# Startup edits and a table of per-stage offsets in the instruction order of a two-layer attention and feed-forward kernel

## The chip, the core and the metric

The kernel runs on one core of one Trainium2 chip. The metric is the device time of one execution in microseconds (us). A program on this core is five instruction queues that run side by side: TensorE (PE in the profile, with its weight loads as PEld), VectorE (DVE), ScalarE (ACT), GpSimd (POOL) and SyncE (SP, which here only issues DMAs). Each queue is worked off in the order in which it was written; an instruction whose inputs are late holds up everything behind it in its own queue.

## What is computed

A sequence of 2048 tokens of width 640 goes through four layers: attention with a memory (A), a feed-forward layer (B), A again, B again, with the same weights both times. Every layer normalises its input first and adds its result to it.

```python
x = A_x
x = x + _A_ref(_layernorm(x, axis=-1), A_wq, A_wk, A_wv, A_wo, A_beta)
x = x + _B_ref(_layernorm(x, axis=-1), B_w1, B_w2)
x = x + _A_ref(_layernorm(x, axis=-1), A_wq, A_wk, A_wv, A_wo, A_beta)
x = x + _B_ref(_layernorm(x, axis=-1), B_w1, B_w2)
# in _A_ref, for each of 4 segments of 512 tokens, 32 heads of width 20:
logits = jnp.einsum('bhqd,bhkd->bhqk', qs, ks) * scale + mask
p = _softmax(logits, axis=-1)
a_dot = jnp.einsum('bhqk,bhkd->bhqd', p, vs)
num = jnp.einsum('bhld,bhde->bhle', pq, M)      # pq = phi(qs), phi(t) = t+1 or exp(t)
den = jnp.einsum('bhld,bhd->bhl', pq, z)[..., None] + 1e-06
o = g * (num / den) + (1.0 - g) * a_dot          # g = sigmoid(beta), one value per head
M = M + jnp.einsum('bhld,bhle->bhde', phi(ks), vs)
z = z + jnp.einsum('bhld->bhd', phi(ks))
```

B is `relu(x @ w1) @ w2` with an inner width of 1728.

## The kernel before

**Tiles and stages.** Tokens lie on the 128 partitions, 16 tiles of 128 tokens (`x_sb`). A stage is named by a layer number a (0 or 1) and a segment s (0 to 3). For each stage the kernel normalises (statistics on DVE, `stats`; the power -0.5 on POOL, `chain`, L700 to L711; the scaling on DVE), turns the tiles so that features lie on partitions (a DMA transpose, `turn`, except for the first segment, which TensorE turns), projects to q, k and v (`proj_part`, `proj_v`), spills q and k to DRAM and loads them back as four heads per group at partitions 0, 32, 64, 96 (`spill`, `fill`), computes scores on TensorE with 20-row tiles (`scores`, L1170, "rows" mode), exponentials on ACT (`exps`, L1235, 128 x 1024 each), the causal mask on POOL (`causal`), the weighted sum of values (`apply`), a DMA transpose and a division on DVE (`divide`, L1359), the memory read and write (`mem_read`, `mem_write`), the sum of the two terms (`combine`, L1388), another DMA transpose (`turn_o`), the output projection (`out_proj`), a second normalisation (`ln_b`, L1442) and the feed-forward layer (`ffn`, `ffn_rest`).

**Who sets the order.** All these stages are Python generators ("streams") that are added in a fixed sequence at L1566 to L1602, so that each has a number n: 0 `scores`, 1 `exps`, 2 `causal`, 5 `turn_pair`, 6 `divide`, 7 `turn_o`, 8 and 9 `out_proj`, 10 and 11 `ln_b`, 12 `fill`, 13 `spill`, 14 `combine`, 15 and 16 `phi_`, 17 and 18 `mem_read`, 19 `turn_k`, 20 `mem_write`, 25 the fourth `first_one`, 26 `first_ln_b`, 27 `proj_ln`, 29 and 30 `proj_one`, 31 `proj_v`, 32 `ffn`, 33 `ffn_rest`, 34 `store`, 36 `consts`, 37 `loads`, 38 `late_loads`. Streams that go through the eight stages carry the rank 4a + s; others keep rank 0. When the program is built, `Sched.run` (L298) repeatedly looks at the next instruction of every stream, estimates with built-in costs when it could start, and appends to its engine's queue the one with the smallest key (L334):

```python
key = (round(start + late), 0.5 if op.urgent else prio, self.rank[id(st[1])], n)
```

`start` is the later of the engine's estimated free time and the inputs' estimated arrival; `late` is a reserve that `_late` (L275) adds from some point on for inputs that have only just come. The order in the queues is fixed by this when the program is built; on the chip only real arrivals count. An engine can't skip an instruction that was appended too early.

**The first 20 us.** Four x tiles are loaded, tiles 0 and 1 by SP, tiles 2 and 3 by ACT. `warm_pe` (L646) runs 52 matmuls of 128 columns on the identity matrix, which POOL has built before. Tiles 0 and 1 get mean and variance on DVE (`first_sums`, L782) and a chain of two POOL instructions each; tiles 2 and 3 get them on ACT (`first_ln_b`, L800: two sums, one mean, two sums of squares), then one DVE instruction that scales the sums (in `chain`, recorded as L708), then the power on POOL. `first_tile` (L756) normalises each tile on DVE, turns it with five TensorE transposes (L764) into a PSUM bank, and copies it out (L771 or L773). Then the projections of the first segment run (L673 in `group`). `MISC` (L484) is four PSUM banks that nearly all stages share.

**Constants.** `consts` (L592) lets POOL build the mask `maskg` (a memset and ten selections), loads beta for all 128 partitions by one SP DMA of 128 rows (L627), takes its exponential on ACT (L630) and derives the gate on DVE (L631 to L641).

Of the kernel before, what the change touches and what calls it, by code (L numbers as in the profile page):

```python
# [5 lines left out]
dt = mybir.dt  # L6
ACT = mybir.ActivationFunctionType
# [3 lines left out]
D = 640  # L11
H = 32
# [160 lines left out]
HOLDERS = 1  # L173
HOLD_TOL = {"pe": 220.0, "act": 150.0, "dve": 200.0, "pool": 0.0, "sp": 0.0}


class Sched:
# [120 lines left out]
    def run(self):  # L298
        while True:
# [24 lines left out]
            for prio, n, st, alts, op, late in heads:  # L324
# [9 lines left out]
                key = (round(start + late), 0.5 if op.urgent else prio, self.rank[id(st[1])], n)  # L334
# [94 lines left out]
def bass_interleave_layers__memory_aug_infini_attn__dense_activation_relu__prompt_kernel(  # L429
    nc, A_x, A_wq, A_wk, A_wv, A_wo, A_beta, B_x, B_w1, B_w2, out,  # L430
):
    with contextlib.ExitStack() as es:
# [13 lines left out]
        ident = sb("ident", [128, 128])  # L446
        warm = sb("warm", [128, 1], dt.float32)
        asum = sb("asum", [128, 4], dt.float32)
        beta_bc = sb("beta_bc", [128, H])
# [3 lines left out]
        stats6 = sb("stats6", [128, 12, 2, 6], dt.float32)  # L453
# [19 lines left out]
        om_sb = sb("om_sb", [128, NJ, D])  # L473
        rden = sb("rden", [128, 2, 2, NJ, 4, 1], dt.float32)
# [58 lines left out]
        def loads():  # L533
# [7 lines left out]
            for t in range(4):  # L541
                yield from ld(("sp", "act")[t // 2], "x0%d%d" % divmod(t, 2), 163840, lambda e, t=t: e.dma_start(
                    x_sb[:, t, :], xs[:, t, :]))
            yield from cols("wk0", wk_r, A_wk, 0, 256)
# [47 lines left out]
        def consts():  # L592
            tw = yield dve(4, 1, lambda e: e.memset(warm[:], 0.0))
            yield act(4, lambda e: e.activation(warm[:], warm[:], ACT.Exp), [tw], psum=False)
            t0 = yield pool(150, lambda e: e.memset(ident[:], 0.0))
            t1 = yield pool(250, lambda e: e.affine_select(
                out=ident[:], in_=ident[:], compare_op=ALU.not_equal, fill=1.0, base=0,
# [16 lines left out]
            t3 = yield pool(700, lambda e: e.memset(maskg[:], 1.0))  # L614
            tmm = []
            for c in range(FC):
# [9 lines left out]
            yield Need("x11")  # L626
            tb = yield dma("sp", sem_("d_beta"), 16384, lambda e: e.dma_start(  # L627
                beta_bc[:], bass.AP(tensor=A_beta.tensor, offset=A_beta.offset, ap=[[0, 128], [1, H]])))
            yield Need("stg", 0, 0, 0, 1)
            te = yield act(32, lambda e: e.activation(gt[:, 0, :], beta_bc[:], ACT.Exp), [tb], psum=False)  # L630
# [14 lines left out]

        def warm_pe():  # L646

            idt = yield Need("ident")
            yield Acq([X])
            tk = yield pe(4600.0, [(lambda e: e.matmul(  # L650
                ps[:, 0, 0:128], ident[:], ident[:], start=True, stop=True), k == 51) for k in range(52)], idt)
            X.release(tk)

# [37 lines left out]
        def stats(t, xt):  # L691
            tk = None
            for c2 in range(2):
                tk = yield dve(320, 1, lambda e, c2=c2: e.bn_stats(  # L694
                    stats6[:, t % 12, c2, :], x_sb[:, t, c2 * 320:(c2 + 1) * 320]), xt)
            tk = yield dve(50, 1, lambda e: e.bn_aggr(
                mv[:, t, :], stats6[:, t % 12, :, :].rearrange("p c s -> p (c s)")), [tk])
# [938 lines left out]
```

## Time and profile before

| What | Value |
|---|---|
| Time, median of 3 runs | 556.43 us (555.3 to 559.99) |
| Span of the profiled execution, first to last instruction | 553.7 us |
| That execution's own time | not listed apart from the three runs: the span is 1.6 us under the lowest and 2.7 us under the median |
| PE busy | 545.7 us, 8340 matmuls |
| DVE / ACT / POOL busy | 414.2 / 408.7 / 191.9 us |
| PE's share of the chain that ended last | 89% |
| Granted TensorE clock, mean | 1.000 |

The span is the time between the first and the last instruction; the times of the runs include what lies around it. A busy PE is not a PE at its peak: every matmul's record includes the time until its result has left the array, about 0.17 us more than what it costs in a dense stream (a 128 x 512 matmul has a mean of 380 ns on the page, and eight of them in a row took 1.89 us at 95.66 us, one every 216 ns).

### The profile page before, as it was taken

The page shows a single profiled execution, that of the slowest core. Times are in us where ns is not written, and L with a number is a line of the kernel's source. Part 1 is how long each engine was busy: PE and PEld are TensorE (multiplying, and loading weights), DVE is VectorE, ACT ScalarE, POOL GpSimd, SP SyncE. Part 2 cuts the span into 40 slices and gives each one's busy share as a digit, 9 for nine tenths or more (in the row PEclk, how much of TensorE's full clock was granted, in tenths as well). Part 3 has the DMA queues.
Part 4 walks back from the last instruction along what each step waited for, and adds up shares of the span by engine and source line. Part 5 has one row for each costly group of instructions (what it writes and reads, how often), then busy time and mean ns, then how long its engine had stood idle before and what let it go on. Part 6 is the DMA issues. An engine that isn't in the chain of part 4 may idle for free.

```text
span 553.7 us, 19086 instructions
## 1 busy us (share of the span) xinstructions
PE 545.7 (99%) x8340; PEld 308.3 (56%) x8340; DVE 414.2 (75%) x1059; ACT 408.7 (74%) x518; POOL 191.9 (35%) x302
## 2 busy tenths in 40 slices
PE   8999999999999999999999999999999999999998
PEld 7464554455564555646446555565456654657756
DVE  5967989897898988997687998669886886417202
ACT  5699889889877888687887887778874878651140
POOL 5245344343444334343433443034430433301000
DMA  8595999933854138466276332971439322342201
GB/s 271 134 232 158 227 186 211 239 72 45 191 112 91 32 58 199 79 93 92 60 188 107 60 69 21 207 147 22 67 48 223 92 36 54 69 81 28 74 2 51
DMA packets 130292, 61.32 MB, mean 111 GB/s; under 512 B 109090, under 2 KB 120098, under 8 KB 130210
## 3 DMA queue, kind: packets, MB, share of 16 engines
q1 hardware_dynamic: 129648, 59.58, 50.8%
q8 instruction: 65, 1.06, 0.8%
q10 hardware_dynamic: 562, 0.53, 0.3%
q14 instruction: 17, 0.14, 0.1%
HBM read 20.57 MB, written 12.85 MB: 60 GB/s over the span
## 4 chain that ended last, share of the span: by engine, by line
PE 89%; DVE 5%; DMA 2%; ACT 2%; POOL 0%; SPq 0%; issue 0%; ACTq 0%; POOLq 0%
PE ps L673 42%; PE ps L676 27%; PE ps L1192 8%; PE ps L1286 6%; ACT PT L1254 2%; PE ps L1325 1%; PE ps L1072 1%; PE ps L650 1%; DMA oT<-o_sb 1%; DMA otk<-otu 1%; PE ps L1466 1%; PE ps L1129 1%; DVE hT L1490 1%; DVE xn_tok L740 1%; DMA beta_bc<-in_A_beta_dram 1%; DVE o_sb L1380 1%
## 5 line engine op out<-in xcount | busy, mean ns | idle before, releaser
L1254 ACT ACTIVATE PT<-ps 128x1024 bf16<-128x1024 f32 x320 | 309.0, 1026 | 58.6 <-PE ps L1192 57.3
L1266 POOL TENSOR_SCALAR_AFFINE_SELECT PT<-PT 128x512 bf16<-128x512 bf16 x256 | 166.6, 669 | 266.8 <-ACT PT L1254 266.7
L673 PE MATMUL ps<-w_r,hT 128*128 128x320 bf16 x488 | 78.5, 300 | 0.0
L1512 DVE TENSOR_TENSOR x_sb<-x_sb,ps 128x320 bf16<-128x320 bf16 (+1 forms) x65 | 31.1, 479 | 48.1 <-PE ps L676 34.1
L676 PE MATMUL ps<-xnT,w_r 128*32 128x512 bf16 x1092 | 64.8, 379 | 0.1
L1192 PE MATMUL ps<-pad 20*128 20x512 bf16 (+3 forms) x1024 | 63.4, 301 | 1.2 <-ACT PT L1254 1.0
L673 PE MATMUL ps<-xnT,w_r 128*128 128x512 bf16 x247 | 60.9, 380 | 0.0
L673 PEld LDWEIGHTS ps<-w_r,hT 128*128 128x128 bf16 x488 | 45.6, 98 | 23.5 <-issue 6.4
L694 DVE BATCH_NORM_STATS2 stats<-x_sb 128x6 f32<-128x320 bf16 x124 | 56.0, 474 | 2.6 <-DMA x_sb<-in_A_x_dram 2.2
L676 PE MATMUL ps<-w_r,hT 128*32 128x320 bf16 (+1 forms) x1428 | 52.4, 294 | 0.0
L1192 PEld LDWEIGHTS ps<-pad 20*128 20x128 bf16 x1024 | 17.8, 92 | 52.2 <-ACT PT L1254 28.1
L1491 ACT ACTIVATE hT<-ps 128x512 bf16<-128x512 f32 x51 | 30.5, 598 | 20.5 <-PE ps L676 19.6
L676 PEld LDWEIGHTS ps<-w_r,hT 128*32 128x32 bf16 x1428 | 37.0, 97 | 10.2
L676 PEld LDWEIGHTS ps<-xnT,w_r 128*32 128x32 bf16 x1092 | 28.3, 97 | 24.6 <-issue 0.5
L1296 DVE CAST otu<-ps 128x512 bf16<-128x512 f32 x50 | 34.2, 684 | 8.7 <-PE ps L1286 8.2
L1490 DVE TENSOR_SCALAR hT<-ps 128x512 bf16<-128x512 f32 x53 | 36.1, 682 | 6.1 <-PE ps L673 4.6
L1408 DVE TENSOR_TENSOR x_sb<-x_sb,ps 128x320 bf16<-128x320 bf16 x64 | 29.6, 477 | 14.7 <-PE ps L676 7.3
L1286 PE MATMUL ps<-PT,v_aug 128*21 128x128 bf16 (+3 forms) x896 | 40.4, 301 | 0.0
L1037 ACT ACTIVATE stg<-stg 128x512 bf16<-128x512 bf16 x50 | 31.6, 635 | 8.5 <-DVE rtmp L1035 8.5
L673 PE MATMUL ps<-wo_r,oT 128*128 128x320 bf16 x234 | 37.0, 300 | 0.3 <-DMA oT<-o_sb 0.3
L710 POOL TENSOR_TENSOR rstd<-lnU,mhalf 128x2 f32<-128x2 f32 (+2 forms) x26 | 20.3, 780 | 47.5 <-DVE lnU L706 37.6
L673 PEld LDWEIGHTS ps<-xnT,w_r 128*128 128x128 bf16 x247 | 22.2, 97 | 25.3 <-issue 3.7
(109 smaller groups left out, 737.2 us busy)
## 6 DMA issues: line engine op xcount, KB each, us to landing
pad<-scr SPq DMA_DIRECT2D x124, 80.0 KB
scr<-stg SPq DMA_DIRECT2D x34, 256.0 KB, 2.9
out_dram<-x_sb SPq DMA_DIRECT2D x15, 160.0 KB, 2.2
w_r<-in_B_w_dram SPq DMA_DIRECT2D x10, 216.0 KB, 2.5
w_r<-in_B_w_dram SPq DMA_DIRECT2D x13, 160.0 KB, 3.0
x_sb<-in_A_x_dram SPq DMA_DIRECT2D x10, 160.0 KB, 3.4
scr<-w_r SPq DMA_DIRECT2D x5, 256.0 KB, 2.9
wv_r<-in_A_wv_dram SPq DMA_DIRECT2D x1, 800.0 KB, 8.8
```

Source lines behind the costliest of these rows:

```text
L673: return e.matmul(view(dst.ap, b), a, b, start=(k == 0), stop=(k == last))
L676: return e.matmul(view(dst.ap[rows], b), part, b, start=(k == 0), stop=(k == last))
L694: tk = yield dve(320, 1, lambda e, c2=c2: e.bn_stats(stats6[:, t % 12, c2, :], x_sb[:, t, c2 * 320:(c2 + 1) * 320]), xt)
L1037: te = yield act(512, lambda e, q=q: e.activation(q, q, ACT.Exp), [tr] + p, psum=False)
L1192: fns.append([(lambda e, z=z, j=j, hh=hh, N=N, o=o, sl=sl, q=hh % 2: e.matmul(slot.ap[:, q, o:o + N], sl.ap[32 * hh:32 * hh + DH, z, 0, 12 ...
L1254: tx = yield act(1024, lambda e, dst=dst, src=src: e.activation(dst, src, ACT.Exp, scale=SCALE), sc + pw)
L1266: tm = yield pool(600.0, lambda e, reg=reg: e.affine_select(out=reg, in_=reg, pattern=[[0, 4], [1, 128]], compare_op=ALU.is_ge, fill=0.0, ...
L1286: fns.append((lambda e, OD, j=j, hh=hh: e.matmul(OD.ap[32 * hh:32 * hh + DH + 1, 128 * j:L], VAUG[vx(a, s)][:, j, 4 * g + hh, :], pt.ap[:, ...
L1296: te = yield evac(L, 1, lambda e: e.tensor_copy(dst, OD.ap), lambda e: e.activation(dst, OD.ap, ACT.Copy), [tk] + OTU[0].tks)
L1490: th = yield evac(512, 1, lambda e: e.tensor_scalar(hT[:, dc, :], bk.ap[:, :], 0.0, None, ALU.max), lambda e: e.activation(hT[:, dc, :], b ...
L1491: lambda e: e.activation(hT[:, dc, :], bk.ap[:, :], ACT.Relu), [tk] + HT.tks)
L1512: ta = yield dve(n, 1, lambda e: e.tensor_tensor(x_sb[:, t, c0:c0 + n], x_sb[:, t, c0:c0 + n], bk.ap[:, 0:n], ALU.add), [tk], urgent=True)
```

## The change

- **Constant run on TensorE.** `warm_pe` no longer waits for the identity from POOL: DVE fills a 128 x 128 corner of the tile `PT` with ones, and 41 matmuls (before: 52) run on that. The turn of tile 0 gets 5 such matmuls more behind its five transposes. The identity now lies in `om_sb` and has no tile of its own.
- **Variance of tiles 2, 3.** The scaling of the sums in `chain` goes from DVE to POOL.
- **beta.** One row of 64 bytes is loaded by an ACT DMA behind the x tiles into a zeroed tile, and one matmul with the ones (output 128 x 32, into a `MISC` bank) spreads it; ACT takes the exponential from that bank. The SP DMA of 128 rows, and the wait that put the exponential behind the first k and q copies, go.
- **Mask.** POOL's memset for `maskg` waits for the scaling of tile 3.
- **Offsets.** A table `SHIFT`, by stream number and rank, is added to the key; 81 entries from -3200 to +3600 ns.
- **Estimates.** Some built-in costs change (a score round 233 for 221 ns, a POOL power of one column 620 for 740 ns), and three DVE instructions are marked as sharing a port with POOL in the estimate. `stats6` has a place for each of the 16 tiles.

```diff
+SHIFT = {
+    (1, 0): 100, (2, 0): 400, (5, 0): -500, (6, 0): 100, (7, 0): -700, (7, 2): 1700, (7, 3): 100, (7, 4): 600,
+    (8, 3): -200, (8, 4): 100, (8, 5): -500, (9, 2): -500, (9, 6): -200, (10, 1): -2700, (10, 2): 200, (10, 3): -100,
+    (10, 4): 200, (10, 6): 600, (10, 7): 300, (11, 2): -2300, (11, 3): -3100, (11, 4): 200, (11, 5): 400,
+    (11, 6): 800, (11, 7): -200, (12, 1): -200, (12, 2): 2500, (12, 3): -400, (12, 4): -1400, (12, 5): 900,
+    (12, 6): -100, (12, 7): -100, (13, 0): -900, (13, 1): -400, (13, 2): 2000, (13, 3): 2000, (13, 5): -200,
+    (13, 7): 3600, (14, 1): 400, (14, 2): -3000, (14, 3): -3000, (14, 6): -1000, (14, 7): -1400, (15, 0): 200,
+    (15, 2): 300, (15, 6): 200, (16, 2): 300, (16, 6): -200, (16, 7): 200, (17, 1): -100, (17, 3): -300,
+    (17, 6): -300, (17, 7): -100, (18, 1): -100, (18, 7): -100, (19, 2): -400, (19, 5): -800, (19, 6): 1400,
+    (20, 2): -200, (20, 4): -800, (20, 5): 100, (20, 6): -400, (25, 0): -600, (26, 0): 1700, (27, 5): 500,
+    (29, 3): 100, (29, 4): -800, (30, 6): -200, (31, 0): -1100, (31, 5): -100, (32, 7): 100, (33, 2): -1600,
+    (33, 3): 100, (33, 4): 100, (33, 5): 400, (33, 6): 500, (34, 4): 500, (34, 7): 900, (36, 0): 100, (37, 0): 800,
+    (38, 0): -3200,
+}
...
-                key = (round(start + late), 0.5 if op.urgent else prio, self.rank[id(st[1])], n)
+                key = (round(start + late + SHIFT.get((n, self.rank[id(st[1])]), 0)), 0.5 if op.urgent else prio, self.rank[id(st[1])], n)
...
+            tz = yield Need("beta0")
+            yield from ld("act", "beta", 64, lambda e: e.dma_start(
+                beta_z[0:1, :], bass.AP(tensor=A_beta.tensor, offset=A_beta.offset, ap=[[H, 1], [1, H]])), tz)
...
-            t3 = yield pool(700, lambda e: e.memset(maskg[:], 1.0))
+            ntk = yield Need("normed", 3)
+            t3 = yield pool(700, lambda e: e.memset(maskg[:], 1.0), ntk)
...
-            yield Need("x11")
-            tb = yield dma("sp", sem_("d_beta"), 16384, lambda e: e.dma_start(
-                beta_bc[:], bass.AP(tensor=A_beta.tensor, offset=A_beta.offset, ap=[[0, 128], [1, H]])))
-            yield Need("stg", 0, 0, 0, 1)
-            te = yield act(32, lambda e: e.activation(gt[:, 0, :], beta_bc[:], ACT.Exp), [tb], psum=False)
+            tb = yield Need("betab")
+            bk, tb = tb[0], tb[1:]
+            te = yield act(32, lambda e: e.activation(gt[:, 0, :], bk.ap[:, 0:H], ACT.Exp), tb)
+            bk.release(te)
...
+        warm_w = PT[:, 0, 0, 0:128]
...
-            idt = yield Need("ident")
+            tw = yield dve(128, 1, lambda e: e.memset(warm_w, 1.0))
+            tz = yield dve(32, 1, lambda e: e.memset(beta_z[:], 0.0))
+            S.set("beta0", tks=[tz])
             yield Acq([X])
-            tk = yield pe(4600.0, [(lambda e: e.matmul(
-                ps[:, 0, 0:128], ident[:], ident[:], start=True, stop=True), k == 51) for k in range(52)], idt)
+            tk = yield pe(107.0 * 41, [(warm_mm, k == 40) for k in range(41)], [tw])
             X.release(tk)
+            tb = yield Need("beta")
+            yield Need("first", 1)
+            bk, tk = yield pe(40.0, [(lambda e, bk: e.matmul(
+                bk.ap[:, 0:H], warm_w, beta_z[:], start=True, stop=True), True)], tb, acq=MISC)
+            PTS[0].tks = [tk]
+            S.set("betab", tks=[bk, tk])
...
-                tk = yield dve(n, 1, lambda e: e.tensor_scalar(lnU[:, sl], sq, 1.0 / D, LN_EPS, ALU.mult, ALU.add), tk)
+                tk = yield pool(190, lambda e: e.tensor_scalar(lnU[:, sl], sq, 1.0 / D, LN_EPS, ALU.mult, ALU.add), tk)
...
-            bk, tT = yield pe(56.0 * FC, fns, [tn] + idt, acq=MISC)
+            if t == 0:
+                fns += [(lambda e, bk: warm_mm(e), False) for _ in range(5)]
+            bk, tT = yield pe(900.0 if t == 0 else 56.0 * FC, fns, [tn] + idt, acq=MISC)
...
-                    return pe(221.0, fns, a[1] + b[1] + a[0].tks + b[0].tks, take=[a[0], b[0]], mode="rows"), None
+                    return pe(233.0, fns, a[1] + b[1] + a[0].tks + b[0].tks, take=[a[0], b[0]], mode="rows"), None
```

## The prediction

> **What bounds the kernel now.** I read the page's first, second and fourth parts, then PE's waits, then the windows, then the timeline of the first 22 us.
>
> ```profile
> span 553.7 us, 19086 instructions
> PE 545.7 (99%) x8340; PEld 308.3 (56%) x8340; DVE 414.2 (75%) x1059; ACT 408.7 (74%) x518; POOL 191.9 (35%) x302
> ...
> PE 89%; DVE 5%; DMA 2%; ACT 2%; POOL 0%; SPq 0%; issue 0%; ACTq 0%; POOLq 0%
> ```
>
> PE is idle for only 553.7 - 545.7 = 8.0 us, and 89% of the chain that ended last is PE's own work. No other engine passes 75%. So a change of order can save what PE idles, not what other engines do.
>
> ```profile
> PE ps L650 <- POOL mhalf L600: 1.6, 1, 1.6
> PE ps L1192 <- ACT PT L1254: 1.0, 3, 0.7
> PE ps L673 <- DVE w_r L872: 0.9, 1, 0.9
> PE ps L673 <- DVE xnT L771: 0.7, 1, 0.7
> PE ps L673 <- DMA oT<-o_sb: 0.3, 1, 0.3
> PE ps L673 <- DVE v_aug L927: 0.3, 1, 0.3
> ```
>
> PE's own waits make 4.8 us, and 1.6 of that lies ahead of the constant run, where no useful work waits. DMA, which the order of SP's queue would cure, stands for 0.3 us.
>
> ```profile
> 20.00:40.00 20.00, 19.34 (x227) 10.34 (x225) 15.99 (x43) 19.13 (x24) 9.38 (x14) 1.00 0.92 222
> 40.00:60.00 20.00, 18.54 (x308) 9.72 (x308) 16.17 (x44) 19.99 (x23) 11.70 (x18) 1.00 0.67 173
> ...
> 300.00:400.00 100.00, 100.00 (x1428) 54.13 (x1428) 82.01 (x212) 81.08 (x102) 37.52 (x57) 1.00 0.43 81
> 400.00:500.00 100.00, 100.00 (x1656) 57.34 (x1658) 62.35 (x161) 67.47 (x86) 27.52 (x42) 1.00 0.41 86
> ...
> 551.00:553.70 2.70, 0.32 (x20) 0.12 (x8) 0.32 (x1) 0.00 (x0) 0.00 (x0) 1.00 0.17 44
> ```
>
> The columns are stretch, length, then busy us of PE, PEld, DVE, ACT, POOL. From 300 to 551 us PE has no gap. The only stretch with much idle is 40 to 60 us (1.46 us), where ACT is full (19.99 of 20). The last 2.4 us are the output's DMA.
>
> ```profile
> 1.59 5.61 PE L650 MATMUL ps<-ident 128*128 128x128 bf16 x52 [1.59 <-POOL mhalf L600]
> 7.04 0.72 PE L764 MATMUL ps<-ident,xn_tok 128*128 128x128 bf16 x10
> 8.46 0.72 PE L673 MATMUL ps<-xnT,wk_r 128*128 128x256 bf16 x5 [0.70 <-DVE xnT L771]
> ...
> 10.17 0.97 PE L764 MATMUL ps<-ident,xn_tok 128*128 128x128 bf16 x10
> ...
> 11.73 0.72 PE L673 MATMUL ps<-xnT,wk_r 128*128 128x256 bf16 x5
> ...
> 21.68 0.40 PE L1192 MATMUL ps<-pad 20*128 20x384 bf16 x8 [0.66 <-ACT PT L1254]
> ```
>
> These are start and length. Useful work on PE begins at 8.46 us. The constant run holds PE to 7.20 (1.59 + 5.61), although DVE had finished tile 0 at 5.66 (its L752 starts at 5.26 and takes 0.40).
>
> The sum is made against the span of 553.7 us. The profiled execution's whole time isn't listed by itself; the span is 2.7 us under the median of 556.43, and I carry a saving over to that median one for one.
>
> **Constant run.** Removed: 52 matmuls at 5.61/52 = 108 ns and the wait for POOL. Added: 41 of them, 4.4 us, behind a DVE memset. DVE's first instruction starts at 0.87, and a memset of 128 columns took 0.17 us (L605), so the run lies at about 1.1 to 5.6. The turn of tile 0 (normalised at 5.66) can then start at 5.8 instead of 7.04; five turns and five constants at 108 ns end near 6.8. Tile 1 isn't ready before 6.84 (L752 at 6.39, 0.45), and nothing in the change moves that. Its turn then ends near 7.4: five at 56 ns, 0.22 for the last to leave the array (the 0.72 of L764 fits 9 x 0.056 + 0.22). The copy of tile 0 by then has run beside it on DVE, so only one copy (0.89/2 = 0.45) follows, and projections start near 7.95 instead of 8.46: -0.5 us. Ends: 0, if tile 0's copy is queued ahead of tile 1's scaling (which then goes back by 0.45), and -0.8, if the first copy is fully out of the way and the waits between shrink too. The second DVE memset and the identity's new place cost nothing on this path: DVE idles until 3.11 for x, and POOL ends the identity near 1.5, against a first use at 5.8.
>
> **Variance of tiles 2, 3.** ACT ends its sums at 7.40 (7.22 + 0.18), but DVE scales them only at 8.32, behind two copies. On POOL that costs 0.2 to 0.3 (L704: 236 ns) and starts near 7.5, so the power (0.71) ends near 8.5 rather than 9.27. Against that, beta's exponential (0.23) may now sit on ACT between these sums, waiting for the end of the constant run at 5.6, and the ACT DMA queue gets one issue more (some 0.45); offset (26, 0) of +1700 ns makes the first more likely. I take 0.4 us earlier, and 0.4 more since POOL's mask memset no longer runs beside the two scalings (1.26 for two, against 0.40 and 0.45 alone). But the 20 projections of the first half (0.109 each, 2.2 us) fill PE until about 10.1 anyway; between 9.89 and 11.73 PE lost at most 0.5 us. I take 0; ends 0 and -0.5.
>
> **beta.** The SP DMA ends at 19.55 and ACT's exponential starts at 19.57 after 1.31 us of idle; the first score exponential follows at 19.71, although its scores were out at 18.65. PE's 0.66 us at 21.02 waits for exactly those. With beta there early, ACT starts about 1 us sooner and the gap closes: -0.7, ends 0 (the freed time meets a full ACT from 20 to 60 us) and -0.7. The new matmul has 32 columns (under 0.1 us); it is queued behind the constant run on PE, ahead of tile 0's turn, so a late beta row would hold PE. The nearest DMA rows are 2.8 us for the old beta and 2.9 for an x tile; issued near 2 us it lands near 5, ahead of 5.6: nothing, with +0.5 as the other end. The removed SP issue (0.48) and the mask's selections, which move from 10 to 14.5 us on POOL, cost nothing: POOL was idle from 13.9 to 20.9.
>
> **Offsets and estimates.** They add no instruction; they move some past others. What they can recover is PE's idle between 40 and 551 us: 1.46 + 0.23 (80 to 100) + 0.38 (100 to 200) + 0.49 (200 to 300) = 2.6 us. What they can cost is bounded under the third rival at +10. Most entries of PE streams are below 0.5 us, so I take a value near the gain's end: a third, -0.8.
>
> Sum: -0.5 + 0 - 0.7 - 0.8 = -2.0 us, 556.4 - 2.0 = 554.4 us. This is a gain of 0.4%.
>
> [...] In this trace TensorE gives a 128-column matmul every 108 ns until about 6.9 us, 5.3 us after its first, and every 56 ns from the turns on. The mean clock column says 1.00 throughout and doesn't show it. [...]
>
> **Rivals.**
>
> 1. *The offsets close everything.* All 2.6 us of idle go, with the 0.5 between the halves and a start at -0.8: -0.8 - 0.5 - 0.7 - 2.6 = -4.6, 551.8 us. For it: PE is the bound and each gap has a single cause. Against it: the ACT-bound stretch from 20 to 60 us keeps its work.
> 2. *The full rate comes later.* If the switch at 6.9 us moves behind the first 20 projections, these cost 213 ns rather than 109 (+2.1) and the five turns of tile 1 108 rather than 56 (+0.3): +2.4 on -2.0, 556.8 us. For it: PE now pauses between 5.6 and 5.8 and between 7.2 and 7.95. Against it: with the five constants behind tile 0's turn PE is busy from 1.1 to 6.8, 5.7 us, as long as before.
> 3. *Instructions queued too early hold DVE* (slower than before). Seven entries move `ln_b` and `combine` forward by 1.0 to 3.1 us: (10,1), (11,2), (11,3), (14,2), (14,3), (14,6), (14,7). Place: DVE between about 90 and 250 us and again above 350, where DVE is 80 to 90% busy. If the transposed attention output comes later than the recorder assumed (otk took 4.85 us at 99.41), DVE waits, and the PSUM copies behind it (0.68 for 512 columns) wait too. PE goes on until the free `MISC` banks are full; a group of five 512-column matmuls lasts 5 x 0.216 = 1.1 us, so two free banks cover 2.2 us, and a 3.0 us hold costs PE 0.8. Three entries of about 3.0 us with four instructions each make 12 x 0.8 = 9.6, some +10 at most. It decides from 2.0 us on, three such holds; half of them give +4.8 - 1.2 (the start's gains) = +3.6, 560.0 us. For it: estimates are fixed, DMAs landed between 3.3 and 6.2 us for one kind. Against it: DMA waits cost PE 0.3 us in all of the trace of before.
>
> **How the numbers follow.** Forecast 0.55, first rival 0.13, second 0.12, third 0.20. The time is the forecast's, 554.4 us. About 1% (5.6 us) is what a measurement of this kernel tells from no change. Below 550.9 lies half of the first rival: faster 0.07. Above 562.0 lie two thirds of the third: slower 0.13. Within 1%: 0.80. The range leaves out about these two tails: 550.5 to 562.0; the forecast alone with its own ends reaches from 551.8 to 556.5.
>
> **What the new profile would show.** The constant run from about 1.1 with 41 matmuls; the first projection near 7.95 (8.3 or later: that step is wrong); the second half's first projection before 11.4; no DMA of beta on the chain and the first 128 x 1024 exponential directly behind its scores; PE's wait for ACT near 21 us gone; PE's idle total below 8.0 - 2.0 = 6.0 us. Projections 213 ns apart would show the second rival. Long DVE idle before L1399 or L694 with PE waiting for DVE copies would show the third. A change of PE's busy time itself by more than 1 us would make the whole sum wrong, since I hold PE's work fixed.

## The result and the profile after

The changed kernel took 558.08 us (median of 20 runs, 555.68 to 561.28) beside 556.14 us for the kernel before (20 runs, 554.68 to 559.99): a ratio of 1.0034, 95% interval 1.0022 to 1.0046. It is 1.9 us slower, where a gain of 2.0 us was forecast: the time lies inside the stated range, but the change went the other way. Its profiled execution has a span of 557.4 us, and the time of the same execution is 559.19 us.

The page of the changed kernel, parts 1 and 4:

```profile
span 557.4 us, 21794 instructions
PE 546.0 (98%) x9697; PEld 312.2 (56%) x9697; DVE 417.9 (75%) x1060; ACT 408.8 (73%) x518; POOL 191.2 (34%) x303
...
PE 83%; DVE 8%; DMA 5%; ACT 2%; issue 0%; SPq 0%; POOL 0%; ACTq 0%
```

PE's busy time looks unchanged (546.0 for 545.7), but it holds the extra time of matmuls at half rate, shown below; a second profile of the same kernel (changed_2, below) has no such stretch behind the start and 543.8. PE's idle time has grown from 8.0 to 11.4 us, and DVE and DMA have a larger part of the chain. The 1357 further matmuls are the same work in narrower pieces: the recorder cuts more groups into 32-column tiles when it finds them another place.

PE's waits in this execution of the changed kernel:

```profile
PE ps L702 <- DVE w_r L904: 1.4, 2, 1.0
PE ps L666 <- DVE warm L610: 1.1, 1, 1.1
PE ps L1224 <- ACT PT L1286: 1.1, 2, 0.9
PE ps L678 <- DMA beta_z<-in_A_beta_dram: 0.9, 1, 0.9
PE ps L1224 <- DMA pad<-scr: 0.7, 1, 0.7
PE ps L705 <- DMA xnT<-xn_tok: 0.7, 1, 0.7
```

The wait for POOL's identity (1.6) has become one of 1.1 for DVE's memset. The waits for beta and for the DMAs vary from one execution to the next: changed_2's profile has none for beta, and 2.7 us in two waits for `pad`.

PE's start in the changed kernel (start, length, instruction, idle before):

```profile
1.12 4.55 PE L666 MATMUL ps<-PT 128*128 128x128 bf16 x41 [1.12 <-DVE warm L610]
6.53 0.21 PE L678 MATMUL ps<-beta_z,PT 128*128 128x32 bf16 x1 [0.86 <-DMA beta_z<-in_A_beta_dram]
6.58 0.69 PE L794 MATMUL ps<-om_sb,xn_tok 128*128 128x128 bf16 x5
...
8.93 1.20 PE L702 MATMUL ps<-xnT,wk_r 128*128 128x256 bf16 x5 [0.59 <-DVE xnT L803]
9.96 0.71 PE L702 MATMUL ps<-xnT,wq_r 128*128 128x256 bf16 x5
...
13.23 0.72 PE L702 MATMUL ps<-xnT,wk_r 128*128 128x256 bf16 x5 [0.59 <-DVE xnT L805]
```

Tile 0 was ready at 5.98, but its turn stands behind the beta matmul, and beta's row landed near 6.5 us. The first projection starts at 8.93 (forecast 7.95, before 8.46). Five of 256 columns in 1.20 us, where the next five take 0.71, show that the full rate came only at about 9.9 us. The second half starts at 13.23 (forecast: before 11.4).

ACT and its DMA queue (ACTq) at the start of the changed kernel:

```profile
1.15 0.90 ACTq L556 DMA_DIRECT2D x_sb<-in_A_x_dram  x2
2.08 0.54 ACTq L559 DMA_DIRECT2D beta_z<-in_A_beta_dram  x1
...
6.71 0.74 ACT L837 ACTIVATE hT<-x_sb 128x640 bf16<-128x640 bf16 x1 [2.01 <-DMA x_sb<-in_A_x_dram]
```

The x loads were issued 0.18 us later than before (0.97), and tile 3's sums began 2.13 us later than before (4.58).

Most of this lateness belongs to this execution and not to the kernel. In changed_2, the same kernel, the loads are issued at 1.15 too, and PE and ACT show:

```profile
5.47 0.23 PE L678 MATMUL ps<-beta_z,PT 128*128 128x32 bf16 x1
...
8.00 0.72 PE L702 MATMUL ps<-xnT,wk_r 128*128 128x256 bf16 x5 [0.59 <-DVE xnT L803]
...
5.61 0.74 ACT L837 ACTIVATE hT<-x_sb 128x640 bf16<-128x640 bf16 x1 [0.91 <-DMA x_sb<-in_A_x_dram]
```

There beta's matmul follows the constants without a wait, the first projection comes at 8.00, the forecast's 7.95, and the second half at 12.12, still later than before (11.73).

Windows of the changed kernel (columns as before, then the granted clock as a fraction, DMA share, GB/s), first two of 20 us, then two of 3.41 us:

```profile
40.00:60.00 20.00, 17.31 (x278) 9.04 (x277) 15.46 (x39) 20.00 (x24) 12.10 (x20) 1.00 0.63 168
60.00:80.00 20.00, 20.00 (x205) 11.41 (x204) 16.50 (x47) 15.20 (x22) 6.80 (x10) 0.91 0.85 204
```

```profile
57.73:61.14 3.41, 1.75 (x14) 0.63 (x17) 3.38 (x9) 3.39 (x4) 2.44 (x4) 1.00 1.00 189
61.14:64.55 3.41, 3.41 (x55) 2.10 (x48) 3.38 (x11) 2.48 (x4) 1.70 (x3) 0.50 0.99 232
```

From 40 to 60 us PE idles for 2.69 us (before 1.46). Then comes something that no step of the forecast had: for 3.41 us the granted clock is 0.50. PE counts as fully busy in it, so the busy share does not show the loss. Half of 3.41 us, 1.7 us, is the most that it can cost; row by row it cost 1.15 us (see "Filling the idle").

### The profile page after: what moved, and what is told of

Its sections match the earlier page's. It is cut to its first block, busy times and chain, and to the rows that moved or that the text cites. A ratio compares the mean times of both kernels' runs of the same rounds, so it can differ in the third digit from the quotient of the medians.

```text
span 557.4 us, 21794 instructions
## 1 busy us (share of the span) xinstructions
PE 546.0 (98%) x9697; PEld 312.2 (56%) x9697; DVE 417.9 (75%) x1060; ACT 408.8 (73%) x518; POOL 191.2 (34%) x303
## 3 DMA queue, kind: packets, MB, share of 16 engines
q8 instruction: 76, 1.25, 0.9%
## 4 chain that ended last, share of the span: by engine, by line
PE 83%; DVE 8%; DMA 5%; ACT 2%; issue 0%; SPq 0%; POOL 0%; ACTq 0%
PE ps L705 38%; PE ps L702 28%; PE ps L1224 7%; PE ps L1318 5%; ACT PT L1286 2%; PE ps L1104 1%; DVE xn_tok L769 1%; DMA oT<-o_sb 1%; DMA xnT<-xn_tok 1%; DMA phk<-phs 1%; DVE o_sb L1412 1%; PE ps L1161 1%; DMA beta_z<-in_A_beta_dram 1%; DMA pad<-scr 1%; PE ps L1357 1%; DVE stats L723 1%
## 5 line engine op out<-in xcount | busy, mean ns | idle before, releaser
L705 PE MATMUL ps<-xnT,w_r 128*32 128x512 bf16 x1500 | 92.2, 379 | 0.0
L705 PE MATMUL ps<-w_r,hT 128*32 128x320 bf16 (+1 forms) x1820 | 67.6, 295 | 0.0
L702 PE MATMUL ps<-w_r,hT 128*128 128x320 bf16 x390 | 62.8, 300 | 0.0
L705 PEld LDWEIGHTS ps<-xnT,w_r 128*32 128x32 bf16 x1500 | 37.5, 97 | 33.6 <-issue 4.1
L705 PEld LDWEIGHTS ps<-w_r,hT 128*32 128x32 bf16 x1820 | 47.4, 97 | 11.9
L702 PEld LDWEIGHTS ps<-w_r,hT 128*128 128x128 bf16 x390 | 36.5, 98 | 18.2 <-issue 4.6
L702 PE MATMUL ps<-xnT,w_r 128*128 128x512 bf16 x145 | 36.2, 380 | 0.2 <-DMA xnT<-xn_tok 0.2
L1328 DVE CAST otu<-ps 128x512 bf16<-128x512 f32 x42 | 28.6, 682 | 6.6 <-PE ps L1318 4.7
L705 PE MATMUL ps<-wo_r,oT 128*32 128x320 bf16 x780 | 33.0, 299 | 0.0
L769 DVE TENSOR_SCALAR xn_tok<-x_sb,mv,rstd 128x640 bf16<-128x640 bf16 x60 | 29.6, 520 | 3.5 <-POOL rstd L739 3.4
```

Source lines behind the costliest of these rows:

```text
L702: return e.matmul(view(dst.ap, b), a, b, start=(k == 0), stop=(k == last))
L705: return e.matmul(view(dst.ap[rows], b), part, b, start=(k == 0), stop=(k == last))
L769: nm = lambda e, bx, t, k: e.tensor_scalar(bx.ap[:, k * D:k * D + D], x_sb[:, t + k, :], mv[:, t + k, 0:1], rstd[:, t + k:t + k + 1], ALU. ...
```

## The experiments

Every execution of a kernel has a span and a mean granted clock. One stretch of 3.41 us at half rate lowers the mean over 557 us by 0.003 (3.41 x 0.5 / 557), so 0.997 is read as one stretch and 0.994 as two: the changed kernel's profile has one and 0.997, beta_later's has two and 0.994. The half rate before the first switch at the start does not enter this mean: the changed kernel's profile reads 1.00 until 9.9 us although its constants are 107 ns apart. Behind the start, matmuls at half rate stand where this record says so: five of 320 columns in 1.49 us, for 0.84, in the changed kernel's stretch at 0.50 (62.47 us), and five of 512 in 2.31, for 1.25, in that of both (58.89 us). All executions, counted by that:

| Kernel | Ratio to before, 95% interval | Clock 1.000: executions, mean span (us) | Clock lower: mean span (us) |
|---|---|---|---|
| before | 1 | 127 of 145, 554.6 | 556.4 |
| changed | 1.0034 [1.0022, 1.0046] | 6 of 20, 555.2 | 556.9 |
| changed_2 (the same kernel) | 1.0024 [1.0004, 1.0043] | 4 of 12, 554.7 | 556.6 |
| beta_later | 1.0018 [1.0002, 1.0034] | 3 of 12, 555.3 | 556.3 |
| warm_first | 1.0030 [1.0011, 1.0050] | 5 of 12, 554.6 | 557.3 |
| both | 1.0028 [1.0009, 1.0046] | 2 of 12, 555.0 | 556.4 |
| both_2 (the same) | 1.0015 [1.0001, 1.0029] | 4 of 12, 555.3 | 555.8 |
| both_busy | 1.0007 [0.9987, 1.0026] | 9 of 12, 554.7 | 556.9 |
| both_busy_2 (the same) | 1.0013 [0.9997, 1.0029] | 8 of 12, 554.7 | 556.6 |
| both_busy_more | 1.0025 [1.0000, 1.0050] | 10 of 12, 555.7 | 559.5 |
| changed_busy | 1.0008 [0.9993, 1.0024] | 10 of 12, 554.5 | 557.0 |
| old_order_pool | 1.0000 [0.9988, 1.0012] | 12 of 12, 554.6 | |
| old_order_short_run | 1.0029 [1.0013, 1.0046] | 8 of 12, 556.4 | 557.0 |
| old_order_short_run_2 (the same) | 1.0017 [1.0001, 1.0032] | 6 of 12, 555.3 | 556.4 |
| old_order_run_fill | 1.0006 [0.9991, 1.0021] | 9 of 12, 555.0 | 555.8 |
| old_order_new_start | 0.9996 [0.9976, 1.0016] | 9 of 12, 553.7 | 557.0 |
| old_order_new_start_2 (the same) | 0.9993 [0.9978, 1.0007] | 10 of 12, 554.0 | 556.1 |
| start_only | 1.0173 [1.0152, 1.0195] | 0 of 4 | 564.2 |
| no_offsets_old_costs | 1.0119 [1.0098, 1.0140] | 0 of 4 | 561.1 |
| old_start_offsets | 1.0394 [1.0373, 1.0415] | 0 of 4 | 576.8 |

The expectations below were written run by run. That the clock column separates the executions of one kernel was seen only before the last two.

### The two late arrivals at the start: beta_later, warm_first, both

beta_later records the beta matmul behind the turn of tile 1:

```diff
             tb = yield Need("beta")
-            yield Need("first", 1)
+            yield Need("xt", 0, 0, 0)
```

> The changed kernel with one edit: the matmul that spreads beta is recorded behind tile 1's turn, so it stands on PE behind both turns; the order of all other instructions on all five queues is that of the changed kernel. Start theory (the loss sits in the first 20 us): PE no longer idles 0.86 us for beta's DMA, tile 0's turn starts near 6.0 instead of 6.58, the full matmul rate comes before the first projections, and the first projection starts at 8.0 to 8.5 instead of 8.93; the second half of them still waits for tile 3 (13.2 us), so the time falls by only 0 to 0.7 us from 558.1. Order theory (the loss sits behind 30 us in the new order of the queues): within 0.3 us of 558.1 and PE's idle behind 30 us unchanged.

warm_first records the one-column memset that ACT's first instruction waits for (`warm`) ahead of the two new ones on DVE:

```diff
-            tw = yield dve(4, 1, lambda e: e.memset(warm[:], 0.0))
+            tw = yield dve(4, 1, lambda e: e.memset(warm[:], 0.0)); S.set("warmset")
...
+            yield Need("warmset")
             tw = yield dve(128, 1, lambda e: e.memset(warm_w, 1.0))
```

> The changed kernel with one edit: DVE clears the one-column tile for ACT's first exponential ahead of the two new memsets instead of behind them; all else keeps its order. ACT's queue waits for that memset before it issues the loads of tiles 2 and 3. Start theory: the loads are issued near 0.97 instead of 1.15, tile 3 lands near 4.6 instead of 6.7, the second half's first projection moves from 13.23 to 11.5 to 12.3, and the time falls by 0.7 to 1.5 us from 558.1. Order theory: the start moves as said, but the gain is used up by 60 us, where ACT is full, and the time stays within 0.4 us of 558.1.

both makes both edits.

> Both edits of the start (beta's matmul behind tile 1's turn, ACT's memset first), the order of all else that of the changed kernel. Start theory: first projection near 8.0, second half near 11, 1.5 to 2.2 us under 558.1, so no slower than the 556.1 of the kernel before. Order theory: 557.3 to 558.1, still slower than before although the start is as early as it was there.

PE's start in beta_later:

```profile
5.82 0.51 PE L794 MATMUL ps<-om_sb,xn_tok 128*128 128x128 bf16 x5
...
8.03 0.72 PE L702 MATMUL ps<-xnT,wk_r 128*128 128x256 bf16 x5 [0.57 <-DVE xnT L803]
```

ACT's start in warm_first:

```profile
0.97 0.87 ACTq L556 DMA_DIRECT2D x_sb<-in_A_x_dram  x2
1.88 0.54 ACTq L559 DMA_DIRECT2D beta_z<-in_A_beta_dram  x1
...
4.97 0.74 ACT L837 ACTIVATE hT<-x_sb 128x640 bf16<-128x640 bf16 x1
```

Each edit does what it was meant to do. Without the beta matmul ahead of it, the turn starts at 5.82 and the first projection at 8.03. With `warm` first, the loads are issued at 0.97 again, tile 3's sums start 1.74 us earlier than in the change's first profile, and the second half's first projection starts at 11.92 instead of 13.23. But changed_2, without either edit, has 8.00, 5.61 and 12.12 in these places: most of what the edits seem to move is the difference between two executions of one kernel. The times hardly move: 1.0018, 1.0030, 1.0028, intervals that all overlap with the change's. My theory that the loss lay in the first 20 us falls as far as its size goes: both was to gain 1.5 us or more and gained 0.4 (all executions of both and both_2 against those of changed and changed_2, 95%: from 1.1 faster to 0.4 slower).

### The offsets and estimates: start_only, no_offsets_old_costs, old_start_offsets

start_only is the changed kernel with `SHIFT = {}`; no_offsets_old_costs also has the old estimates (221 ns for a round, 740 for the power, without the two port marks that the change adds); old_start_offsets is the kernel before with only the table and the key.

> The changed kernel with an empty table of offsets; all other edits stay, so every queue's order behind the first 20 us is a third one, neither that of before nor that of the changed kernel. Start theory: the start still loses, 557.3 to 558.5. Order theory: the offsets are what costs, 555.5 to 556.5 or faster, near the kernel before.

> The changed kernel with an empty table and the old built-in costs and port marks: only the edits of the start are left, and the order that the old rules give them. If the changed costs made the 566 of the empty table, this is back at 555.5 to 558. If any small shift of the estimates throws the order about, it may be anywhere from 556 to 568, and PE's idle time between 40 and 80 us tells which.

> The kernel before with the table of offsets and nothing else. If the offsets are good in themselves, 554 to 556. If they only fit the one recording that they were found for (the run with an empty table took 566), they do harm here: 558 to 568, with PE idle in one or two long pieces between 30 and 100 us.

PE's largest wait in old_start_offsets, then in start_only:

```profile
PE ps L1206 <- ACT PT L1268: 8.5, 9, 2.0
```

```profile
PE ps L1224 <- ACT PT L1286: 4.8, 5, 2.0
```

The table costs 22 us on the start it was not made for, more than either of its expectations allowed. The new start without it loses 6.6 us with the old estimates and 9.6 with the new ones; for the latter both expectations were missed. None of these numbers is the price of the offsets. An edit at the start changes the recorder's estimated times, and the order of the whole kernel is dealt anew (PE gets 9234 matmuls in old_start_offsets, 8554 in start_only, 8482 in no_offsets_old_costs, 9697 in the changed kernel and 8340 in the one before); the table mends this one dealing. A step of such a kernel can therefore not be undone alone: the waits that come up (8.5 us on ACT) belong to a third order.

### The start in the old order: old_order_new_start, old_order_short_run, old_order_run_fill, old_order_pool

These leave the estimates of the kernel before as they were, so that the order behind the start stays. old_order_short_run has only the 41 matmuls on ones; old_order_run_fill also the 5 behind tile 0's turn; old_order_pool has the 52 matmuls, and the scaling of tiles 2 and 3 on POOL with the mask behind tile 3; old_order_new_start has all of it, with beta as before.

```diff
-            idt = yield Need("ident")
+            yield Need("warmset"); ones = PT[:, 0, 0, 0:128]
+            tw = yield dve(128, 1, lambda e: e.memset(ones, 1.0))
...
-                tk = yield dve(n, 1, lambda e: e.tensor_scalar(lnU[:, sl], sq, 1.0 / D, LN_EPS, ALU.mult, ALU.add), tk)
+                tk = yield pool(190, lambda e: e.tensor_scalar(lnU[:, sl], sq, 1.0 / D, LN_EPS, ALU.mult, ALU.add), tk)
```

> The kernel before with the start edits only: 41 constants on ones without the wait for POOL, five more behind tile 0's turn, the scaling of tiles 2 and 3 on POOL, the mask behind tile 3's scaling; beta stays as it was, ACT's memset stays first, and the order of all other instructions on all queues is that of the kernel before. Start theory (what the start gains or loses reaches the end): first projection near 8.0 instead of 8.46, second half near 11 instead of 11.73, and 0.4 to 1.2 us under the kernel before. Order theory (the stretch from 20 to 60 us, where ACT is full, decides, and the start only moves idle time into it): within 0.3 us of the kernel before.

> The kernel before with one edit: 41 constants on ones that DVE writes, without the wait for POOL, in place of 52 on the identity; every other instruction in its old place. Clock theory (the shorter run delays the full matmul rate): turns and first projections at half rate, 109 becoming 213 ns, first projection later than 8.46, 0.3 to 1.5 us over the kernel before. Start theory: first turn near 6, first projection near 8.0, 0 to 0.5 us under the kernel before.

> The kernel before with 41 constants on ones and five more behind tile 0's turn, all else in its old place; it differs from old_order_short_run (557.8) in the five alone. Clock theory (without the five, PE idles 0.94 and 0.72 us ahead of the projections and the rate is halved again in part of the executions): 555.5 to 556.6. If that run was slow for another reason: 557 to 558.

> old_order_short_run once more, for a second profile and a second set of times. Clock theory: again 0.5 to 2 us over the kernel before, and in some profile the projections near 8 to 12 us 213 ns apart. If the first result was chance: within 0.6 us of the kernel before.

> The kernel before with the scaling of tiles 2 and 3 on POOL and the mask behind tile 3's scaling, and nothing else; the run of 52 stays. Second half's first projection 0.5 to 1.0 us earlier than 11.73. Start theory: 0 to 0.5 us under the kernel before. Order theory: within 0.3 us.

> The order of before, with the 41 constants, the 5 behind tile 0's turn, the scaling of tiles 2 and 3 on POOL and the mask behind tile 3; beta as before, no offsets. The same kernel as the earlier one of that name. There 9 of 12 executions at a clock of 1.000 had a mean span of 553.7, against 554.6 for the kernel before at 1.000. Theory (the start is a gain of about 0.9 us, and the earlier ratio of 0.9996 hid it behind three halved executions): executions at 1.000 near 553.7 again, ratio 0.9980 to 0.9995. Rival (the start is worth nothing): executions at 1.000 within 0.3 us of the kernel before, ratio 0.9995 to 1.001.

PE's start in the second old_order_new_start:

```profile
1.15 4.55 PE L650 MATMUL ps<-PT 128*128 128x128 bf16 x41 [1.15 <-DVE PT L648]
5.99 0.71 PE L764 MATMUL ps<-ident,xn_tok 128*128 128x128 bf16 x5 [0.29 <-DVE xn_tok L752]
...
8.20 0.72 PE L673 MATMUL ps<-xnT,wk_r 128*128 128x256 bf16 x5 [0.58 <-DVE xnT L771]
```

Over both sets, 19 of 24 executions have a clock of 1.000 and a mean span of 553.9 (95%: 553.5 to 554.2) against 554.6 for the kernel before: the start is worth -0.8 us there. The ratios of 0.9996 and 0.9993 hold the five others as well; over all 24 the gain is 0.4 us, with an interval from 1.0 faster to 0.2 slower. The shorter run alone is a loss (1.0029 and 1.0017, executions at lower clock in 10 of 24); with the five behind the turn it is none (1.0006). Why it costs even where the clock is 1.000 (556.4 and 555.3) stays open. The projections at half rate that the clock theory expected are in neither of its profiles; compared row by row, both are ahead of the kernel before at 8 us and behind it by 3.2 and 2.0 us at 106 us, which they lose in waits after the start. The POOL edit alone is worth nothing, 1.0000, and its second half starts at 11.49, only 0.24 us earlier for the 0.5 to 1.0 expected. So neither part gains by itself (old_order_run_fill 555.0, old_order_pool 554.6, before 554.6 at a clock of 1.000); together they do (553.9).

### Filling the idle: both_busy, changed_busy

Four matmuls of 512 columns with zero weights are added ahead of the last matmul of one q projection of segment 1, near 57 us. They add zero to a running sum: the result is unchanged, PE has 0.9 us more work (four of 512 columns; in changed_busy they start at 55.66 and the next matmul at 56.52). One more memset on DVE, at the start, writes the zeros.

```diff
-                    fns = [(lambda e, bk=bk, mm=mm: mm(e, bk), k == last)]
+                    fns = [(lambda e, bk=bk, b=b: e.matmul(view(bk.ap, b), hR[:, 0:128], b, start=False, stop=False), False)
+                           for _ in range(zeros * (k == last))] + [(lambda e, bk=bk, mm=mm: mm(e, bk), k == last)]
```

both_busy puts them into both, changed_busy into the changed kernel itself. both_busy_more adds to both_busy 7 constants at the start and puts 10 behind each of the turns of tiles 0 and 1 (in both_busy: 5 behind tile 0's, none behind tile 1's). changed_2 and both_2 repeat those kernels on the same chip as both_busy_2.

> The changed kernel with both edits of the start, and four matmuls more with zeros as weights, added into the sum of one q projection of segment 1 ahead of its last matmul (near 56.3 us, just before PE's idle pieces of 0.86 and 0.96 us); the result is the same and the order of all else stays. Clock theory (PE's idle pieces near 57 to 59 us make the matmul rate halve for 3.4 us, and this is most of what the new order costs): no halved stretch near 60 us, five projections at 59 us take 1.25 instead of 2.31 us, and the time falls by 1.0 to 1.7 us from the 557.4 of the run without them, to 555.7 to 556.4. Order theory (the loss is spread over waits and changes of tile shape): 557 to 558, since 1.7 us at one place is not what separates the two kernels.

> The changed kernel as it is, on the chip and against the runs of before that the next three share. Both theories: 1.002 to 1.0046 times the kernel before; it is the measure for the other three.

> The run 'both' once more. Clock theory: 0.3 to 0.9 us under changed_2, since only the start is mended and the halved stretch near 60 us stays. Start theory: 1.3 us or more under changed_2, the whole of what the start lost in the trace.

> The run 'both_busy' once more. Clock theory: another 0.6 to 1.5 us under both_2 and within 0.4 us of the kernel before. If the four matmuls with zeros do nothing: within 0.3 us of both_2.

> As both_busy, with 48 constants for 41 and ten behind each of the turns of tiles 0 and 1 (five behind tile 0's before), in PE's idle time, so that the start too has no idle stretch over 0.7 us; the order of all else stays. Clock theory: no halved stretch at 8 to 12 us, 0.3 to 1.0 us under both_busy_2, so 0 to 1 us under the kernel before. If the start's rate doesn't reach the end: within 0.3 us of both_busy_2.

> The changed kernel with nothing altered but four matmuls with zero weights (512 columns, they add zero to a sum that is already running) ahead of the last matmul of the second q projection of segment 1, near 57 us. They cost four times 0.216 = 0.9 us of PE and lie in a stretch where PE otherwise waits for ACT. Over both sets of executions of the changed kernel, 22 of 32 show a mean granted clock under 1.000 and take 556.8 us of span, the other 10 take 555.0; the kernel before shows it in 16 of 120 (556.5 against 554.6). Theory of the halved rate (the two waits near 57 us bring the halving, and the halving makes most of the loss): at most 5 of 12 executions under 1.000, a mean span of at most 555.6, ratio 1.000 to 1.0015. Rival (the new order and the start cost it by themselves, the clock only follows): as many as without the four matmuls, 7 or more of 12, and a ratio of 1.0024 to 1.0034.

The stretch in question, PE in the changed kernel:

```profile
58.43 0.39 PE L1224 MATMUL ps<-pad 20*128 20x512 bf16 x4 [0.86 <-ACT PT L1286]
59.78 1.25 PE L702 MATMUL ps<-hT,wq_r 128*128 128x512 bf16 x5 [0.96 <-DVE w_r L904]
...
62.47 1.49 PE L702 MATMUL ps<-wv_r,hT 128*128 128x320 bf16 x5
...
68.25 0.84 PE L702 MATMUL ps<-wv_r,hT 128*128 128x320 bf16 x5
```

and in changed_busy:

```profile
55.66 1.03 PE L713 MATMUL ps<-hT,hR 128*128 128x512 bf16 x4
56.52 0.38 PE L702 MATMUL ps<-hT,wq_r 128*128 128x512 bf16 x1
56.90 0.39 PE L1224 MATMUL ps<-pad 20*128 20x512 bf16 x4
58.26 1.25 PE L702 MATMUL ps<-hT,wq_r 128*128 128x512 bf16 x5 [0.97 <-DVE w_r L904]
...
60.80 0.84 PE L702 MATMUL ps<-wv_r,hT 128*128 128x320 bf16 x5
```

The zero matmuls (L713) fill the wait for ACT, the one for DVE stays, and five projections of 320 columns take 0.84 us instead of 1.49. Executions below a clock of 1.000 fall from 22 of 32 (both sets of the changed kernel) to 2 of 12, and the mean span from 556.3 to 554.9, that of the kernel before. More work on PE makes the kernel 1.4 us shorter (95%: 0.5 to 2.3). With the start mended the count falls as well, from 18 of 24 in both to 7 of 24 in both_busy, but the time gains less: 0.6 us, with an interval from 1.3 faster to 0.1 slower. In the two that were measured side by side, both_2 and both_busy_2, the count falls from 8 to 4 of 12 and the ratio only from 1.0015 to 1.0013, so the 0.6 to 1.5 us that I expected there were missed. In the first profiled execution of both_busy the remaining half rate lies in another place, behind the constant run: the granted clock is 0.91 from 0 to 10 us, 0.92 from 10 to 20, and 1.00 from there to 551. both_busy_more thinned that out as well (2 of 12), but its executions at 1.000 are 1.0 us longer (555.7): my expectation was missed; that the fillers cost more than they saved is the likely reason, but not shown.

changed_2 gave the control. It is the changed kernel, its profiled execution has the same two waits, and no halving:

```profile
57.52 0.39 PE L1224 MATMUL ps<-pad 20*128 20x512 bf16 x4 [0.86 <-ACT PT L1286]
58.87 1.25 PE L702 MATMUL ps<-hT,wq_r 128*128 128x512 bf16 x5 [0.96 <-DVE w_r L904]
...
61.42 0.84 PE L702 MATMUL ps<-wv_r,hT 128*128 128x320 bf16 x5
...
66.19 0.84 PE L702 MATMUL ps<-wv_r,hT 128*128 128x320 bf16 x5
...
69.54 0.40 PE L1224 MATMUL ps<-pad 20*128 20x512 bf16 x4 [1.74 <-DMA pad<-scr]
```

The two executions have the same instructions in the same order, so they can be compared row by row. changed_2 is 0.91 us ahead at the first of these rows (57.52 for 58.43), which it owes to the start, and 2.06 ahead behind the stretch (66.19 for 68.25): the halved stretch cost 1.15 us. A wait of 1.74 us for a DMA then takes nearly all of the lead; the 1.7 us between the two spans (555.7 and 557.4) come from other waits further on.

## Why the prediction was wrong

**What holds.** The constant run lies where it was put (1.12 to 5.47) and costs 107 ns a matmul. The first projection comes at 8.00 in one of the kernel's two profiles and at 8.03 in beta_later, for 7.95. In the old order the start's edits without beta's are worth -0.8 us at a clock of 1.000, where -0.5 was forecast; but the run and its five alone gain nothing there, and POOL's edit, taken as 0, is worth 0 only by itself. That PE's busy time comes out the same (546.0 for 545.7) is luck: without a halved stretch it is 543.8.

**The beta step's second sentence held in one profile and failed in the other**: "issued near 2 us it lands near 5, ahead of 5.6: nothing". In the first profile, issued at 2.08, it let PE go on at 6.53, 4.4 us later, where the durations it was taken from were 2.8 and 2.9. In changed_2, issued at 2.07, it was there when the constants ended, and PE went on at 5.47. Of the six profiles in which this matmul stands ahead of the turns, PE waited for beta in two, 0.86 us here and 0.57 in changed_busy; "+0.5 as the other end" is about what it cost where it came. The first sentence holds: exponentials now follow their scores, and PE's wait near 21 us is gone. ACT in the changed kernel's first profile, whose first scores start at 19.75 on PE:

```profile
15.90 0.19 ACT L646 ACTIVATE gt<-ps 128x32 f32<-128x32 f32 x1
...
20.18 1.02 ACT L1286 ACTIVATE PT<-ps 128x1024 bf16<-128x1024 f32 x1
```

But those first scores came at 19.75, and in changed_2 at 18.64, where the kernel before has them at 18.25, and the end that I had named at 0 fits: the time freed meets an ACT that is full from 40 to 60 us (20.00 of 20). That it is this that takes the gain is argued and not shown by itself.

**A move that I did not cost** was DVE's `warm`, which two new memsets push back from first place to third. ACT's first instruction waits for it, and ACT's loads of tiles 2 and 3 are issued behind that: `warm` is written from 1.03 to 1.09 us and the loads are issued at 1.15, in warm_first from 0.87 to 0.93 and at 0.97. I costed the "second DVE memset" at nothing because DVE idles; what is queued on ACT behind the wait I did not look at. What the 0.18 us in issuing cost in landing is not shown: tile 3's sums began 2.13 us later than before in the first profile and 1.03 in changed_2 with the same issue.

**The offsets step failed in sign**: "I take a value near the gain's end: a third, -0.8." This is the step that decides. I took PE's idle of 2.6 us between 40 and 551 us as what order could recover and did not price the order before as a good one. That idle grew: it is 4.6 us in the changed kernel's first profile, 5.6 in changed_2 and 3.7 in both. Over all executions both and both_2, with the mended start, take 1.4 us more than the two sets of old_order_new_start, which have the old order (95%: 0.6 to 2.2). The new order and beta's new way together are thus worth about +1.4 us, where -0.8 and -0.7 were forecast. Up to 0.8 us of it may still lie in the start, since the second half comes at 11.95 and 11.81 in one pair and at 11.14 and 11.16 in the other; the two terms are not told apart. In the stretch near 57 us the kernel before has one long wait, for a copy into `w_r`:

```profile
55.59 0.82 PE L673 MATMUL ps<-hT,wq_r 128*128 128x512 bf16 x3 [0.88 <-DVE w_r L872]
```

In the new order there are two, 0.86 and 0.96 us (the second for the same copy), that end 1.4 us apart.

**And the second rival came true in another place.** "The full rate comes later" was priced once, at the start (+2.4, 556.8 us). At the start of the first profile it came at 9.9 us and cost five projections 0.5 us (1.20 for 0.71); in changed_2 the first five, at 8.00, already ran at it (0.72). The larger part is that the full rate is lost again, in the first profile at 61 us. The sum over all executions: the changed kernel's mean span is 556.3, before 554.9, +1.4. Of these, (22/32 - 18/145) x (556.8 - 555.0) = 0.56 x 1.8 = 1.0 us is the greater share of executions with halved stretches. The other 0.4 is the difference at a clock of 1.000 (555.0 against 554.6), with an interval from -0.1 to +0.9: start and order together are worth about nothing there, where -2.0 was forecast, and how the start's gain is lost among beta, `warm` and the new order is not told apart by these runs. changed_busy shows the first part by taking it away: 2 of 12 executions are left with a halved stretch. In which places the stretches lie in the executions without a profile is not known.

The third rival does not apply: DVE's waits for the transposed attention output make 2.5 us in two places (before: 5.2 in two), not 3.0 us twelve times. In the stretch of the two waits DVE is held once, 1.13 us at 55.2 for `rstd`, with the copy for the 0.96 us wait behind it; the kernel before has a hold of the same length and cause there, up to 53.74.

The 1.0 us is a mean over executions with and without a halved stretch. A single pair of profiles, 557.4 and 553.7, would have put the halved stretch and the late start into every execution.

## What to carry to other kernels

Gaps on the bounding engine had two prices here: their own length, 0.86 and 0.96 us, and in one of two profiles of the same kernel a stretch of 3.41 us at a clock of 0.50 behind them, which cost 1.15 us more. So list the gaps by place, not only in sum, and look at the granted clock of many executions before believing one profile; and take a second profile of the same kernel before a late landing is called a cause. If a DMA's landing gates an engine's queue, put what needs it behind the work that does not, and cost every instruction that moves back in any queue by what waits behind it there.

## What the runs showed of the hardware

The halved stretches behind the start last 3.41 us in three profiles: at 61.14 us in the changed kernel's first, at 58.66 in both, at 36.70 and 60.59 in beta_later; start_only's 0.74 from 60 to 80 us makes 10.4 us at half rate, about three of them. The single ones fit a grid of 3.41 us, at another place in each of the three executions: the two in beta_later are 23.89 us apart, seven steps, and the one in the changed kernel comes 51.2 us, fifteen steps, behind the full rate at the start (about 9.9). In changed_2, both_2 and warm_first, which show no halved stretch behind the start, the place of the grid is my estimate, counted in such steps from the full rate at the start (in warm_first between 5.50, where beta's matmul still took 0.23, and 6.21, where five transposes took 0.45). In these six profiles, which all have both waits, it went by the grid: where one of its windows held most of both, the next one was halved (changed, both, beta_later: 1.66, 1.59 and 1.67 us idle); where a window's edge divided them, it was not (changed_2, both_2, warm_first: at most 0.97, 1.06 and 0.95 us idle in one window). changed_2, whose two windows each hold one wait, and both, whose one window holds both:

```profile
54.10:57.51 3.41, 2.56 (x60) 1.50 (x52) 2.27 (x7) 3.41 (x5) 2.57 (x5) 1.00 0.60 167
57.51:60.92 3.41, 2.44 (x38) 1.16 (x39) 3.38 (x8) 3.14 (x4) 2.38 (x4) 1.00 1.02 207
```

```profile
55.25:58.66 3.41, 1.82 (x29) 0.59 (x25) 3.23 (x7) 3.41 (x5) 2.37 (x5) 1.00 0.66 166
58.66:62.07 3.41, 3.18 (x27) 1.11 (x28) 2.76 (x8) 1.85 (x3) 1.67 (x3) 0.50 1.01 226
```

In 3.41 us, an idle of 0.85 and of 0.97 (changed_2) was followed by a clock of 1.00, one of 1.59 (both) and of 1.66 (changed) by 0.50. These runs give no sharp threshold: in beta_later a window with 0.96 idle was followed by a halved one, in changed_2 one with 1.74 was not. Nor does the grid give the number of halved executions: from the start of the first wait to the end of the second it is 2.2 us (57.57 to 59.78 in the changed kernel), so a grid of random phase would hold both in one window in about a third of them, (3.41 - 2.2)/3.41, an estimate from these rows; a lower clock is seen in 22 of 32. Halved stretches in other places, like the one at 36.70 us in beta_later, may make up the rest; how many there are is not shown.

The other surprise was how far the landing of a load moves from one execution to the next while the weights' loads are under way (DMA share of the first 10 us: 0.84 in before, changed and changed_2). With two loads issued at 1.15, the sums that need the second of them began at 5.61 and 6.71 us in two profiles of one kernel (changed_2, changed); issued at 0.97, at 4.58 (before) and 4.97 (warm_first).
